# Fused RWKV attention, Mish MLP and greedy MoE on one core: the attention bonus of units 6 to 23 moved from TensorE to VectorE, with a new order of steps

## The chip, the cores and the metric

One core of one Trainium2 chip runs the whole program as a single launch. The metric is device time in microseconds (us), the median of several runs. Engines are named as the profile names them: PE is TensorE (PEld its weight loads), DVE is VectorE, ACT is ScalarE, POOL is GpSimd, SP is the engine that issues most DMAs.

## The reference, cut to what matters

```python
# attention: r, k, v, w are (4 batches, 8 heads, 768 steps, 48), u is (8, 48)
for t in range(S):
    cur = einsum('bhd,bhe->bhde', u[None] * kt, vt)
    y[:, :, t] = einsum('bhd,bhde->bhe', rt, state + cur)
    state = wt[..., None] * state + einsum('bhd,bhe->bhde', kt, vt)
# MLP on x = y as 3072 tokens of 384 features
h = x @ w_in                        # 384 -> 2048
g = h * tanh(softplus(h))
x = g @ w_out                       # 2048 -> 384
# MoE: greedy assignment of tokens to 8 experts, 384 tokens each,
# by falling logit of x @ w_gate, then per expert relu(x @ w1) @ w2
```

The part of y that `cur` gives is the bonus: for one token and one head it is the scalar sum over d of r·u·k, times v of the same token. The change is about how that scalar is computed.

## The kernel before, in words

**Attention.** The 768 steps of a pair of batches are cut into 12 chunks of 64 steps, and a unit is one chunk of one pair: 24 units (`n` from 0 to 23) of 128 tokens and 8 heads. r, k and w arrive with the head dimension on the partitions (`rkw`, 48 of each 64 partitions used), v with the tokens on the partitions (`v`). Steps of a unit: `att0` (a scan of the decay on VectorE, and the product rk = r·k), `att1` (key "r1": a second scan, and r scaled), `att1b` ("k1": k scaled), `bon1` and `bon2` (the bonus), `att_A` ("A1": the 64x64 scores into PSUM, and the masked copy of them over the bonus matrix `Dt`), `att_K` ("K": transposes of k), `att_S` ("S": the state), `att4` ("y": scores times v, then x0 and its remainder written as two f16 halves into `xg`, and the loads of later units).

**The bonus before.** `bon1` multiplies rk by u on TensorE (8 products of 64 columns, which the trace counts as 16 matmuls), one row of PSUM per head, and copies the 128x128 block to `bT`. `bon2` transposes that block on TensorE, copies the 8 useful columns to `bt` (tokens on the partitions), and spreads bt over a diagonal into `Dt`.

**MLP.** Two units make a group of 256 tokens (12 groups). `mm1(g, j)` is slot t = 8g + j: 18 matmuls of 256 columns into a PSUM tile `Hp` (two buffers). ACT reads each tile twice (tanh into `es`, a copy into `hs`; a few copies go to DVE). A half group (4 slots) of `es` then goes through arctan ("at") and sine ("sin") on ACT, `act_he` on DVE multiplies h by the result, and `act_g` writes the high f16 half (on ACT or DVE, by list) and the low half (DVE). `es` has two buffers: the tanh of a half waits until `act_he` of the half before the last has read them. `mm2` is a stream of 384 parts, each 3 matmuls of 384 or 392 columns, handed out between the slots.

**Weights at the start.** w_in and w_out arrive as 64-bit floats in 16 blocks; `conv` (three integer operations on DVE) makes f32 of a block, `split` (one ACT, one DVE) two f16 halves. `og_T` and `og_M` multiply w_out by the gate weights, so that mm2 gives the gate logits as well. `warm(n)` issues n matmuls whose result nobody reads.

**The order.** Every step is an event with a number as its key: the list `CFG` gives the number for each kind of step, the events are sorted by it, and every engine works through its own instructions in that program order. Slot t of mm1 has the key t + 0.689. For units from 6 on, the keys of units n and n+1 repeat every 8 slots. From slot 16 to 81 `beat` says how many mm2 parts follow slot t (by t mod 8). The sets in `CFG['dve']` say which copies run on DVE; the others run on ACT. SP issues nearly all DMAs, in program order, and holds each until its buffer is free.

**After the MLP.** The greedy gate (a chain of short DVE and PE steps, with the last mm2 parts between them), then the eight experts.

```python
t0 = 8 * (n // 2) - 8 if n >= 6 else 4 * n - 13
for nm, o in {**(CFG["u"][n % 2] if n >= 6 else {}), **CFG["un"].get(n, {})}.items():
    at(t0 + o, steps[nm], n)
...
for key, _, f, args in sorted(events, key=lambda x: x[:2]):
    f(*args)
```

Of the kernel before, what the change touches and what calls it, by code (L numbers as in the profile page):

```python
# [23 lines left out]
CFG = {'conv': [-28.468, -27.682, -10.675, -9.847, -2.299, 2.231, 3.277, 4.9, 3.919, 5.933, 7.595, 7.755, 8.526, 9.471,  # L24
          10.454, 11.547],
 'split': [-25.675, -27.076, -3.646, 1.639, 1.676, 2.567, 3.66, 7.281, 4.908, 7.502, 8.011, 9.047, 9.415, 10.573,
           10.811, 12.671],
 'ogT': [5.845, 8.719, 9.555, 9.756, 11.048, 11.752, 12.058, 13.442],
 'ogM': [7.704, 9.381, 9.717, 10.657, 11.711, 12.133, 12.863, 15.308],
 'u': ({'att0': -6.475,  # L30
        'bon1': -2.417,
        'bon2': -1.013,
        'r1': 0.465,
        'k1': -1.596,
        'K': 1.584,
        'A1': 2.502,
        'S': 3.903,
        'y': 3.747},
       {'att0': -2.581,
        'bon1': -0.459,  # L40
        'bon2': 0.009,
        'r1': -0.43,
        'k1': 0.751,
        'K': 5.062,
        'A1': 5.181,
        'S': 5.915,
        'y': 5.938}),
 'un': {0: {'att0': -24.666,
            'r1': -16.321,
            'bon1': -15.996,  # L50
            'k1': -21.723,
            'K': -15.816,
            'A1': -14.582,
            'bon2': -15.13,
            'S': -15.595,
            'y': -13.813},
        1: {'att0': -20.054,
            'r1': -19.91,
            'bon1': -18.88,
            'k1': -18.572,  # L60
# [3 lines left out]
            'S': -16.313,  # L64
            'y': -15.386},
        2: {'att0': -21.397,
            'r1': -20.207,
            'bon1': -20.059,
            'k1': -19.864,
            'bon2': -3.587,  # L70
            'K': 4.356,
            'A1': 3.2,
            'S': 6.8,
            'y': 7.301},
        3: {'att0': -21.601,
            'r1': -18.499,
            'bon1': -0.615,
            'k1': -16.885,
            'bon2': 2.966,
            'K': 3.773,  # L80
            'A1': 6.657,
            'S': 6.652,
            'y': 7.118},
        4: {'K': 5.178,
            'A1': 4.914,
            'S': 5.604,
            'y': 8.165,
            'att0': 0.318,
            'bon1': 1.82,
            'bon2': 4.604,  # L90
            'r1': 3.684,
            'k1': 4.536},
        5: {'y': 7.557,
            'att0': -2.858,
            'bon1': 3.509,
            'bon2': 3.642,
            'r1': 3.498,
            'k1': 1.649,
            'K': 6.184,
            'A1': 5.986,  # L100
            'S': 6.749},
        6: {'att0': -3.536, 'bon1': -2.54, 'bon2': 0.136},
        7: {'att0': -2.822, 'bon1': -0.422, 'bon2': 1.839}},
 'rate': [(17, 1), (16, 18), (77, 192), (80, 194), (96, 224), (99, 245)],
 'beat': (16, 82, (8, 3, 1, 1, 1, 0, 3, 5)),
 'close_cv': 15.533,
 'close_att': 86.65,
# [11 lines left out]
           ('ld', 5): -25.319,  # L119
           ('ld', 6): -18.857,  # L120
           ('ld', 7): -23.785,
           ('ld', 8): -21.26,
# [1 line left out]
           ('warm', 1): -24.585,
           ('warm', 2): -22.903,
           ('warm', 3): -6.441,
           ('warm', 4): 9.117,
           ('warm', 5): 2.921,
# [26 lines left out]
def tile_rwkv_mish_greedy_moe(  # L155
# [185 lines left out]
    def att0(n):  # L341
        if n > 2 and UN[n - 3][1] + 1 < NCH:
            need(("S", n - 3))
        if n > 1:
# [907 lines left out]
def lay_out(x):  # L1252
# [67 lines left out]
```

## Time and profile before

| What | Value |
|---|---|
| median of 3 runs | 784.49 us (783.0 to 786.48) |
| the profiled execution's own time | 783.24 us |
| its span, first to last instruction | 781.5 us |
| PE busy | 733.1 us (94%) |
| DVE busy | 556.6 us (71%) |
| ACT busy | 411.0 us (53%) |
| granted TensorE clock, mean | 0.981 |

The busy shares are averages over stages that have different limits: loading and converting weights while attention starts, a long stretch in which attention and MLP run side by side, the gate, and the experts. What the change is worth is read stage by stage.

### The profile page before, as it was taken

The page shows a single profiled execution, that of the slowest core. Times are in us where ns is not written, and L with a number is a line of the kernel's source. Part 1 is how long each engine was busy: PE and PEld are TensorE (multiplying, and loading weights), DVE is VectorE, ACT ScalarE, POOL GpSimd, SP SyncE. Part 2 cuts the span into 40 slices and gives each one's busy share as a digit, 9 for nine tenths or more (in the row PEclk, how much of TensorE's full clock was granted, in tenths as well). Part 3 has the DMA queues.
Part 4 walks back from the last instruction along what each step waited for, and adds up shares of the span by engine and source line. Part 5 has one row for each costly group of instructions (what it writes and reads, how often), then busy time and mean ns, then how long its engine had stood idle before and what let it go on. Part 6 is the DMA issues. An engine that isn't in the chain of part 4 may idle for free. (4 is left out here: it accounts for less than half of the span.)

```text
span 781.5 us, 20165 instructions
## 1 busy us (share of the span) xinstructions
PE 733.1 (94%) x8807; PEld 517.0 (66%) x8807; DVE 556.6 (71%) x1054; ACT 411.0 (53%) x689; POOL 57.0 (7%) x98
## 2 busy tenths in 40 slices
PE   3977699999999999999999999999979999999996
PEld 2656576878777787777777765555556666666663
DVE  8999996978788887978777446777745664446620
ACT  3365875576774667667576781110024565445621
POOL 0000000000000000000000010000031223312211
PEclk9998899999999999999999999999989999999999
DMA  8852331323133141322210005100525644456100
GB/s 335 247 181 60 125 97 26 68 42 86 45 67 60 40 94 41 70 57 47 53 27 13 5 14 180 22 21 12 183 74 182 213 150 162 167 200 212 52 31 30
DMA packets 22220, 74.12 MB, mean 95 GB/s; under 512 B 4496, under 2 KB 13072, under 8 KB 20080
## 3 DMA queue, kind: packets, MB, share of 16 engines
q1 hardware_dynamic: 19056, 63.35, 27.7%
q0 software_dynamic: 3072, 9.44, 3.8%
q8 instruction: 71, 1.16, 0.6%
q14 instruction: 21, 0.17, 0.1%
HBM read 62.15 MB, written 9.44 MB: 92 GB/s over the span
## 5 line engine op out<-in xcount | busy, mean ns | idle before, releaser
L561 PE MATMUL Hp<-xg,wi 128*128 128x256 f16 x1728 | 210.4, 277 | 3.9 <-ACT wi L504 1.9
L616 PE MATMUL X<-wo,g 128*128 128x392 f16 (+1 forms) x1152 | 211.0, 328 | 0.0
L561 PEld LDWEIGHTS <-wi 128*128 128x128 f16 x1728 | 167.8, 99 | 33.3 <-ACT wi L504 2.1
L616 PEld LDWEIGHTS <-g 128*128 128x128 f16 x1152 | 107.2, 98 | 63.5 <-issue 0.9
L565 ACT ACTIVATE es<-Hp 128x512 f32<-128x512 f32 x96 | 57.4, 597 | 112.8 <-PE Hp L561 80.0
L1167 PE MATMUL X<-a,hT 128*128 128x384 f16 x576 | 97.2, 326 | 0.0
L1150 PEld LDWEIGHTS <-a 128*128 128x128 f16 x612 | 57.8, 98 | 37.2 <-issue 1.2
L1167 PEld LDWEIGHTS <-hT 128*128 128x128 f16 x576 | 56.4, 98 | 34.8
L1150 PE MATMUL Hp<-xe,a 128*128 128x384 f16 (+1 forms) x468 | 74.7, 314 | 0.7 <-DVE xe L1131 0.4
L588 DVE TENSOR_TENSOR hs<-hs,es 128x1024 f32<-128x1024 f32 x48 | 57.6, 1218 | 17.8 <-ACT es L580 17.6
L601 DVE TENSOR_TENSOR g<-hs,g 128x1024 f16<-128x1024 f32 x48 | 58.7, 1224 | 13.1 <-ACT g L329 12.1
L1095 DVE SCALAR_TENSOR_TENSOR a<-stg,a 128x384 f16<-128x384 f32 (+1 forms) x112 | 63.9, 607 | 0.0
L1092 ACT ACTIVATE a<-stg 128x384 f16<-128x384 f32 (+1 forms) x112 | 56.9, 561 | 0.8 <-DMA stg<-in_w_dram 0.8
L1170 ACT ACTIVATE or<-X 128x384 f32<-128x384 f32 x24 | 11.8, 491 | 81.0 <-issue 60.7
L1155 DVE SCALAR_TENSOR_TENSOR hT<-Hp,hT 128x384 f16<-128x384 f32 x48 | 26.4, 551 | 38.7 <-ACT hT L1154 38.7
L1131 DVE SCALAR_TENSOR_TENSOR xe<-cn,xe 128x384 f16<-128x384 f32 x24 | 13.2, 553 | 56.4 <-ACT xe L1130 56.4
L580 ACT ACTIVATE es<-es,right 128x1024 f32<-128x1024 f32 x48 | 53.3, 1153 | 0.2
L329 ACT ACTIVATE x1o<-X 128x384 f32<-128x384 f32 x19 | 9.4, 493 | 81.2 <-PE X L616 41.6
L329 ACT ACTIVATE hs<-Hp 128x512 f32<-128x512 f32 x77 | 46.0, 598 | 9.0 <-DVE g L601 9.0
L573 ACT ACTIVATE es<-es,mid__124 128x2048 f32<-128x2048 f32 x24 | 48.1, 2003 | 0.4
L1116 POOL DMA_INDIRECT xr<-x_dram,idx x24 | 27.5, 1146 | 119.6 <-DVE idx L1067 111.4
L273 ACT ACT_TABLE_LOAD x26 | 33.4, 1283 | 1.2 <-PEq L1304 0.8
(190 smaller groups left out, 881.1 us busy)
## 6 DMA issues: line engine op xcount, KB each, us to landing
stg<-in_w_dram SPq DMA_DIRECT2D x16, 1536.0 KB, 6.8
T<-in_rkw_dram SPq DMA_DIRECT2D x42, 289.5 KB, 4.9
g<-in_w_out_dram SPq DMA_DIRECT2D x8, 768.0 KB, 5.8
v<-in_v_dram SPq DMA_DIRECT2D x24, 192.0 KB, 3.1
x_dram<-x1o SPq DMA_DIRECT2D x48, 96.0 KB, 2.2
g<-in_w_in_dram SPq DMA_DIRECT2D x4, 768.0 KB, 7.9
wo<-in_w_in_dram SPq DMA_DIRECT2D x4, 768.0 KB, 11.6
xg<-xg SPq DMA_DIRECT2D x72, 16.0 KB, 1.9
```

The lines of the kernel that those rows point to most:

```text
L329: nc.scalar.activation(dst, src, AF.Copy, scale=scale)
L561: nc.tensor.matmul(h[:, fi, :], wi[:, a, kk, f * P:(f + 1) * P], xg[g][:, b, kk, :], start=(n == 0), stop=(n == 3 * KD - 1))
L565: nc.scalar.activation(es[g, hf][:, 2 * q:2 * q + 2, :], h, AF.Tanh, scale=0.5 / (SX * SWI))
L573: nc.scalar.activation(e, e, AF.Arctan, scale=-0.5, bias=mid_)
L580: nc.scalar.activation(e, e, AF.Sin, scale=-2.0, bias=right)
L588: nc.vector.tensor_tensor(h, h, e, op=ALU.mult)
L601: (nc.vector if on_v("glo", 2 * H_ + q) else nc.gpsimd).tensor_tensor(gt[:, 1, sl], h, gt[:, 0, sl], op=ALU.subtract)
L616: nc.tensor.matmul(x, gt[:, a, ff, m * P:(m + 1) * P], wo[:, b, f, 0:n], start=(f == 0 and i == 0), stop=(f == NF - 1 and i == 2))
L1092: nc.scalar.activation(dst[:, 0], src, AF.Copy, scale=sc_)
L1095: nc.vector.scalar_tensor_tensor(dst[:, 1], src, sc_, dst[:, 0], op0=ALU.mult, op1=ALU.subtract)
L1150: nc.tensor.matmul(ps[:, cs], a1[:, a, kk, f * P:(f + 1) * P], x[:, b, kk, cs], start=(n == 0), stop=(n == 3 * KD - 1))
L1167: nc.tensor.matmul(ps, h[:, a, f, ms], a2[:, b, f, :], start=(n == 0), stop=(n == 3 * NF2 - 1))
```

## The change

Units 0 to 5 keep the bonus as it was. For units 6 to 23 r and k are fetched a second time, now with the tokens on the partitions, u comes spread over all 128 partitions (`ur`), and DVE forms r·k, times u, and sums each head's 48 numbers. `bon1` does nothing for these units, and `att0` makes no rk. The buffer of the fetched pair is single (`bufs=1`): unit n+1 is fetched once unit n has been summed. v comes out of the same array as r and k. Nearly every key of the order is new; the sets of copies on DVE change as shown. The keys of single steps are left out below but for the bonus of the later units.

```diff
- 'u': ({'att0': -6.475,
-        'bon1': -2.417,
-        'bon2': -1.013,
...
-       {'att0': -2.581,
-        'bon1': -0.459,
-        'bon2': 0.009,
...
+ 'u': ({'att0': -5.987,
+        'bon1': -2.919,
+        'bon2': -1.132,
...
+       {'att0': -3.2,
+        'bon1': -0.255,
+        'bon2': 0.362,
...
- 'beat': (16, 82, (8, 3, 1, 1, 1, 0, 3, 5)),
+ 'beat': (16, 82, (8, 2, 1, 1, 0, 0, 3, 7)),
...
- 'warm': [3, 0, 3, 21, 0, 2, 8],
- 'amount': {'I0': 3, 'I1': 0, 'c': 3, 'g': 1, 'o': 20, 't': 5},
+ 'warm': [10, 0, 3, 17, 4, 2, 16],
+ 'amount': {'I0': 3, 'I1': 0, 'c': 3, 'g': 1, 'o': 26, 't': 5},
...
-         'Dt': {4, 5, 6, 7, 8, 9, 10, 12, 13, 14, 15, 16, 17, 18, 19, 20, 21, 22, 23},
-         'kn': {10, 14},
+         'Dt': {4, 5, 6, 7, 8, 9, 10, 12, 13, 14, 15, 16, 17, 18, 19, 20, 22, 23},
+         'kn': set(),
...
-         'x0': {0, 4, 5, 6, 7, 8, 9, 10, 11, 12, 13, 14, 15, 16, 17, 18, 19, 21, 22, 23},
-         'bT': {9, 6, 14},
-         'wT': {13, 17, 19, 21, 23}},
+         'x0': {0, 5, 7, 9, 11, 13, 15, 17, 19, 21, 23},
+         'bT': {17, 21, 7},
+         'wT': {13, 14, 16, 17, 19, 21, 22}},
...
+ 'nb': 6}
...
-        nc.sync.dma_start(vt[n], v[n])
+        nc.sync.dma_start(vt[n], rkv[n, :, 2])
...
-    u_T = pa.tile([P, NP, 2, 32], F32, name="u_T", bufs=1)
-    nc.sync.dma_start(u_T.rearrange("p a h b -> p (a h b)"), u)
+    uw = pa.tile([P, H * D], F32, name="uw", bufs=1)
+    u_T = uw[:, 0:NP * 64].rearrange("p (a h b) -> p a h b", a=NP, h=2)
+    nc.sync.dma_start(uw[:, 0:NP * 64], u)
+    rkn = {}
+
+    def load_rk(n):
+        if NB <= n < NU:
+            if n == NB:
+                nc.sync.dma_start(uw, ur)
+            rkn[n] = pa.tile([P, 2, H * D], F32, name="rk", bufs=1)
+            nc.sync.dma_start(rkn[n].rearrange("p a (h d) -> p a h d", h=H), rkv[n, :, 0:2])
...
-        rk = pa.tile([P, NP, C], F32, name="rk", bufs=1)
-        nc.vector.tensor_tensor(rk, Tps["r", n], Tps["k", n], op=ALU.mult)
-        rks[n] = rk
+        if n < NB:
+            rk = pa.tile([P, 2, H * D], F32, name="rk", bufs=1).rearrange("p a c -> p (a c)")[:, 0:NP * C]
+            rk = rk.rearrange("p (a c) -> p a c", a=NP)
+            nc.vector.tensor_tensor(rk, Tps["r", n], Tps["k", n], op=ALU.mult)
+            rks[n] = rk
...
     def bon1(n):
+        if n >= NB:
+            return
...
     def bon2(n):
+        if n >= NB:
+            x = rkn[n]
+            nc.vector.tensor_tensor(x[:, 0], x[:, 0], x[:, 1], op=ALU.mult)
+            nc.vector.tensor_tensor(x[:, 0], x[:, 0], uw, op=ALU.mult)
+            bt = pa.tile([P, 2, NP], F32, name="bt")
+            for j in range(2):
+                nc.vector.tensor_reduce(bt[:, j], x[:, 0].rearrange("t (p j d) -> t j p d", p=NP, j=2)[:, j], op=ALU.add,
+                                        axis=AX.X)
+            rkn.pop(n)
+            load_rk(n + 1)
+            bonus_diag(n, bt)
+            return
         pb = pq.tile([P, C], F32, name="Y", bufs=2)
         made.add("whole")
         nc.tensor.transpose(pb, bTs.pop(n), ident)
         bt = pa.tile([P, 2, NP], F32, name="bt")
         move("bT", n, bt, pb.rearrange("t (p j) -> t j p", j=32)[:, 0:2, :])
+        if n == NB - 1:
+            load_rk(NB)
+        bonus_diag(n, bt)
+
+    def bonus_diag(n, bt):
         bt = bt.rearrange("t j p -> t (j p)")
```

In the new order the events of one pair of units (here 12 and 13, slots 38 to 41; `he 8 1` is half 8, second quarter) read: y 11 (37.918), k1 12 (38.448), bon2 12 (38.868), g 7 1 (39.512), r1 13 (39.874), r1 12 (40.131), k1 13 (40.314), bon2 13 (40.362), he 8 0 (40.527), he 8 1 (40.643), mm1 40 (40.689). Before they read: y 11 (37.938), k1 12, bon2 12 (38.987), g 7 1, r1 13, bon2 13 (40.009), he 8 0, r1 12, he 8 1 (40.525), mm1 40 (40.689), k1 13 (40.751).

## Rows read from the trace of the kernel before

**Rows 1.** Windows by stage: length, then busy time of PE, PEld, DVE, ACT, POOL, clock, DMA.

```profile
0.00:107.00 107.00, 75.51 (x1188) 56.81 (x1189) 101.35 (x166) 58.64 (x117) 1.73 (x10) 0.90 0.58 185
107.00:121.65 14.65, 14.15 (x308) 12.42 (x306) 14.18 (x23) 14.05 (x18) 0.00 (x0) 1.00 0.26 58
121.65:412.44 290.79, 289.82 (x4266) 221.63 (x4263) 236.41 (x368) 189.12 (x272) 0.00 (x0) 1.00 0.25 55
```

**Rows 2.** Timeline of PE, one pair of units: start, length, what.

```profile
252.18 0.43 PE L374 MATMUL Y<-rk,u_T 128*32 128x64 f32 x16
252.54 2.14 PE L561 MATMUL Hp<-xg,wi 128*128 128x256 f16 x18
...
256.35 2.14 PE L561 MATMUL Hp<-xg,wi 128*128 128x256 f16 x18
258.32 0.27 PE L381 MATMUL Y<-ident,bT 128*128 128x128 f32 x1
258.43 1.66 PE L616 MATMUL X<-wo,g 128*128 128x392 f16 x9
...
266.92 4.14 PE L616 MATMUL X<-wo,g 128*128 128x392 f16 x24
...
275.98 0.28 PE L561 MATMUL Hp<-xg,wi 128*128 128x256 f16 x1
```

**Rows 3.** Groups by line, whole run: count, busy us, mean ns, idle before.

```profile
L353 DVE TENSOR_TENSOR rk<-T 128x512 f32<-128x512 f32 x24 | 16.0, 667 | 0.5 <-DMA T<-in_rkw_dram 0.5
...
L460 DVE TENSOR_TENSOR S<-S,F 128x384 f32<-128x384 f32 x20 | 11.2, 558 | 0.7
...
L885 DVE TENSOR_REDUCE best<-Vs 128x24 f32<-128x192 f32 x1 | 0.4, 354 | 0.0
...
L1050 DVE TENSOR_REDUCE sl<-scn 128x24 int32<-128x192 f32 x1 | 0.6, 615 | 0.0
...
L327 DVE TENSOR_SCALAR xg<-A 128x512 f16<-128x512 f32 x20 | 13.7, 686 | 1.9 <-PE A L473 1.8
```

**Rows 4.** Window of one pair, 240.91 to 274.88 us: columns as in rows 1.

```profile
240.91:274.88 33.97, 33.77 (x509) 26.14 (x508) 29.07 (x48) 21.10 (x29) 0.00 (x0) 1.00 0.31 60
```

**Rows 5.** Timeline of DVE in that pair.

```profile
258.60 0.76 DVE L480 SCALAR_TENSOR_TENSOR xg<-A,xg 128x256 f16<-128x256 f32 x2
259.27 0.68 DVE L397 TENSOR_TENSOR T<-T,F 128x512 f32<-128x512 f32 x1
...
262.54 0.20 DVE L358 RECIPROCAL first<-F 128x8 f32<-128x8 f32 x1
...
264.66 0.68 DVE L327 TENSOR_SCALAR hs<-Hp 128x512 f32<-128x512 f32 x1
...
271.01 1.22 DVE L588 TENSOR_TENSOR hs<-hs,es 128x1024 f32<-128x1024 f32 x1
```

**Rows 6.** Timeline of ACT in that pair.

```profile
272.32 0.60 ACT L565 ACTIVATE es<-Hp 128x512 f32<-128x512 f32 x1 [3.57 <-DVE hs L588]
```

**Rows 7.** Timeline of SP in that pair.

```profile
259.38 4.71 SPq L486 DMA_DIRECT2D xg<-xg  x6
```

**Rows 8.** The page's DMA issues: count, KB each, us to landing.

```profile
g<-in_w_out_dram SPq DMA_DIRECT2D x8, 768.0 KB, 5.8
v<-in_v_dram SPq DMA_DIRECT2D x24, 192.0 KB, 3.1
```

**Rows 9.** Timeline of PE, start of the run and the last mm2 parts of the gate.

```profile
2.01 1.46 PE L339 MATMUL Y<-id 128*128 128x512 f16 x3 [2.01 <-DVE id L281]
6.85 0.66 PE L374 MATMUL Y<-rk,u_T 128*32 128x64 f32 x16 [3.38 <-DVE rk L353]
...
562.14 5.04 PE L616 MATMUL X<-wo,g 128*128 128x384 f16 x30
```

**Rows 10.** Timeline of DVE at the end of the weight conversion.

```profile
108.55 1.23 DVE L350 TENSOR_TENSOR_SCAN F<-T,first 128x520 f32<-128x520 f32 x1
...
111.41 0.95 DVE L505 SCALAR_TENSOR_TENSOR wo<-cv,wo 128x768 f16<-128x768 f32 x1
```

More of the change, by code (lines that the diff above doesn't have):

```diff
@@ L21 @@
 SEQ = 768
-CFG = {'conv': [-28.468, -27.682, -10.675, -9.847, -2.299, 2.231, 3.277, 4.9, 3.919, 5.933, 7.595, 7.755, 8.526, 9.471,
+CFG = {'conv': [-28.468, -28.233, -10.675, -9.847, -3.389, 2.249, 3.447, 4.661, 4.089, 5.933, 7.237, 7.743, 8.526, 9.495,
           10.454, 11.547],
[L26 to L29, printed above, removed]
- 'u': ({'att0': -6.475,
-        'bon1': -2.417,
-        'bon2': -1.013,
[L33 to L38, printed above, removed]
-       {'att0': -2.581,
-        'bon1': -0.459,
-        'bon2': 0.009,
[L42 to L57, printed above, removed]
@@ new lines @@
+ 'split': [-26.085, -27.173, -3.643, 0.741, 1.676, 2.651, 3.66, 6.008, 4.915, 7.723, 8.006, 9.047, 9.486, 10.78,
+           10.805, 12.671],
+ 'ogT': [5.759, 8.781, 9.555, 10.425, 11.079, 11.844, 11.926, 13.193],
+ 'ogM': [7.758, 9.334, 9.771, 10.781, 11.786, 12.209, 12.731, 15.188],
+ 'u': ({'att0': -5.987,
+        'bon1': -2.919,
+        'bon2': -1.132,
+        'r1': 0.131,
+        'k1': -1.552,
+        'K': 2.028,
+        'A1': 2.608,
+        'S': 3.787,
+        'y': 3.844},
+       {'att0': -3.2,
+        'bon1': -0.255,
+        'bon2': 0.362,
+        'r1': -0.126,
+        'k1': 0.314,
+        'K': 4.482,
+        'A1': 5.149,
+        'S': 5.569,
+        'y': 5.918}),
@@ L58 @@
+ 'un': {0: {'att0': -24.617,
+            'r1': -16.818,
+            'bon1': -16.145,
+            'k1': -21.676,
+            'K': -15.719,
+            'A1': -14.474,
+            'bon2': -15.081,
+            'S': -15.546,
+            'y': -13.72},
+        1: {'att0': -20.203,
             'r1': -19.91,
-            'bon1': -18.88,
-            'k1': -18.572,
+            'bon1': -18.764,
+            'k1': -18.426,
             'K': -16.839,
@@ L63 @@
             'bon2': -18.264,
[L64 to L83, printed above, removed]
@@ L84 @@
-        4: {'K': 5.178,
-            'A1': 4.914,
-            'S': 5.604,
[L87 to L102, printed above, removed]
@@ L103 @@
-        7: {'att0': -2.822, 'bon1': -0.422, 'bon2': 1.839}},
- 'rate': [(17, 1), (16, 18), (77, 192), (80, 194), (96, 224), (99, 245)],
- 'beat': (16, 82, (8, 3, 1, 1, 1, 0, 3, 5)),
- 'close_cv': 15.533,
+            'S': -16.335,
+            'y': -15.249},
+        2: {'att0': -21.418,
+            'r1': -19.974,
+            'bon1': -19.617,
+            'k1': -19.64,
+            'bon2': -3.61,
+            'K': 4.997,
+            'A1': 3.276,
+            'S': 6.922,
+            'y': 7.451},
@@ new lines @@
+        3: {'att0': -21.269,
+            'r1': -17.288,
+            'bon1': -0.568,
+            'k1': -15.337,
+            'bon2': 3.561,
+            'K': 3.783,
+            'A1': 6.667,
+            'S': 6.009,
+            'y': 7.234},
+        4: {'K': 5.214,
+            'A1': 4.95,
+            'S': 5.604,
+            'y': 7.836,
+            'att0': 0.608,
+            'bon1': 1.856,
+            'bon2': 4.294,
+            'r1': 3.706,
+            'k1': 4.57},
+        5: {'y': 7.485,
+            'att0': -2.727,
+            'bon1': 3.512,
+            'bon2': 3.756,
+            'r1': 3.755,
+            'k1': 1.907,
+            'K': 6.014,
+            'A1': 5.811,
+            'S': 6.972},
@@ L107 @@
+        6: {'att0': -2.91, 'bon1': -1.909, 'bon2': -0.152},
+        7: {'att0': -1.529, 'bon1': -0.364, 'bon2': 0.748}},
+ 'rate': [(17, 1), (16, 18), (79, 187), (80, 182), (96, 211), (98, 233)],
+ 'beat': (16, 82, (8, 2, 1, 1, 0, 0, 3, 7)),
+ 'close_cv': 15.882,
  'close_att': 86.65,
  'mm1': 0.689,
[7 rows of a table removed]
[7 rows of a table added]
  'begin': {('warm', 0): -39.92,
@@ L118 @@
            ('ld', 4): -26.686,
[L119 to L122, printed above, removed]
+           ('ld', 5): -25.313,
+           ('ld', 6): -16.304,
+           ('ld', 7): -23.746,
+           ('ld', 8): -20.836,
            ('ld', 9): -20.908,
[L124 to L128, printed above, removed]
+           ('warm', 1): -24.627,
+           ('warm', 2): -20.713,
+           ('warm', 3): -7.535,
+           ('warm', 4): 6.922,
+           ('warm', 5): 0.758,
            ('warm', 6): 3.3},
- 'warm': [3, 0, 3, 21, 0, 2, 8],
- 'amount': {'I0': 3, 'I1': 0, 'c': 3, 'g': 1, 'o': 20, 't': 5},
+ 'warm': [10, 0, 3, 17, 4, 2, 16],
+ 'amount': {'I0': 3, 'I1': 0, 'c': 3, 'g': 1, 'o': 26, 't': 5},
  'dve': {'lg': set(),
@@ L158, in tile_rwkv_mish_greedy_moe @@
     rkw: bass.AP,
-    v: bass.AP,
+    rkv: bass.AP,
     u: bass.AP,
+    ur: bass.AP,
     w_in: bass.AP,
@@ L168, in tile_rwkv_mish_greedy_moe @@
     nc = tc.nc
-    NU, C, H, D = v.shape
+    NU, C, _, H, D = rkv.shape
     L = C // 2
@@ L214, in tile_rwkv_mish_greedy_moe @@
     UN = [divmod(n, NCH) for n in range(NU)]
+    NB = CFG["nb"]
     vt = {}
@@ L1286, in lay_out @@
         "rkw": np.concatenate([units(x["w"], 1.0, 1), units(x["r"], 0.0, 0), units(x["k"], 0.0, 0)], axis=2),
-        "v": x["v"].reshape(B // 2, 2, H, NCH, L, D).transpose(0, 3, 1, 4, 2, 5).reshape(NU, C, H, D),
+        "rkv": np.stack([x[a].reshape(B // 2, 2, H, NCH, L, D).transpose(0, 3, 1, 4, 2, 5).reshape(NU, C, H, D)
+                         for a in "rkv"], axis=2),
         "u": u.reshape(P, NP * 64),
+        "ur": np.broadcast_to(x["u"].reshape(1, H * D), (P, H * D)),
         "w_in": w_in,
```

6 lines of the change are left out of this document (3 added, 3 removed), and 18 rows, old and new, of the table CFG.

## The prediction

> **What bounds the kernel now.** I read the windows by stage first, because the shares of the page mix stages with different limits. Up to 107 us DVE works 101.35 of 107 us while PE works 75.51: the start hangs on VectorE, which converts the weights. From 107 to 121.65 us all three engines are nearly full. From 121.65 to 412.44 us, where attention and MLP run side by side, PE is busy 289.82 of 290.79 us at the 2.4 GHz level (granted clock 1.00), DVE 236.41 (81%), ACT 189.12 (65%) [rows 1]. Behind that stand the end of the MLP, the gate and the experts, in which no unit's bonus runs.
>
> A modelled end can make PE look full, so the second view is the timeline of PE, by its starts. A slot of mm1 goes from 256.35 to 258.32 us: 18 matmuls of 256 columns in 1.97 us, 109 ns each, where 256 columns at 2.4 GHz are 107 ns. There is no gap to hide in: what is taken out of PE's queue between 121.65 and 412.44 us moves everything behind it forward, as long as PE is not made to wait for something else. The Trainium skill, page "Trainium Kernel Development and Optimization", section "Performance Expectations", says the opposite of trusting that row: matmul busy time is a bad measure, the busy share of weight loads a good one. That share is 221.63 of 290.79 us, 76%, here; by it a quarter of the stretch would be slack and the removal could be hidden, which is the third rival below. The starts, 109 ns apart, speak against it.
>
> **What is removed from PE.** The 16 matmuls of `bon1` start at 252.18 and the next work at 252.54 us: 0.36 us. The transpose of `bon2` starts at 258.32 and the next work at 258.43: 0.11 us [rows 2]. Together 0.47 us for a unit, and 18 units lose both: 18 x 0.47 = 8.5 us. Sixteen of these lie in the full stretch; units 6 and 7, by their old keys (13.46 and 15.58), lie just ahead of it, between 107 and 121.65 us, where PE is busy 14.15 of 14.65 us [rows 1], so I count them too. Bounds: 16 units, 7.5 us; 18 units, 8.5 us.
>
> The copies bT and bt leave ACT, which is no limit at 65%, and leave the PSUM tiles Y to K and S. I count nothing for it.
>
> **What is added to DVE.** For each unit two products of 384 elements and two sums of 192. The product is priced by the 384-element product of `att_S`, 558 ns; the sum by the reduction of 192 elements to 24, 354 ns; one other reduction of 192, with strides and an integer result, took 615 ns and is the upper bound. Added: 2 x 0.558 + 2 x 0.354 = 1.82 us (2.35 at the upper bound). Removed: rk, 0.67 us [rows 3]. Net 1.16 us a unit, 2.3 us a pair. For 7 of the even units behind unit 6 the x0 copy (0.69 us, rows 3) goes to ACT, so a pair gains 1.6 us of DVE work: 29.07 us of 33.97 before [rows 4] becomes about 30.7 of 33.0, 93%. So VectorE still fits, but its waits must shrink from 4.9 to 2.3 us a pair. The skill's "VectorE: DVE Perf Modes", section "Rules for kernel authors", speaks against the change: it calls `tensor_reduce` the slowest DVE operation and advises to keep operations few. The row of 354 ns, against 558 ns for twice the elements in a product, does not show a reduction slower than a product of its size; the rule's side of it is the upper bound above.
>
> **Where DVE can hold PE.** The tight place of a pair is ahead of mm1 of slot 42. There ACT waited 3.57 us, until 272.32 us, for `act_he` (the `es` buffer), then read the Hp tile in 0.60 us [rows 6], and a second time, which I take as long; `act_he` itself ended at 272.23 [rows 5]. PE wanted that tile at 275.98 us [rows 2]. Some 2.5 us were spare.
> In the new order, counted from the end of unit 11's x0 remainder (258.60 + 0.76 = 259.36 us, rows 5), DVE does k1 (0.68), the sums of bon2 12 (1.82), its Dt (0.69), a low half (1.22), a copy of hs (0.68), two r1 (2 x 2.12, from 262.54 to 264.66), k1 (0.68): 10.0 us to the first product of bon2 13. Then 1.82 + 0.69, and two `act_he` of 1.22: 15.0 us, so 274.3 instead of 272.23 us, and the Hp tile is free at 275.5. (All durations are those of rows 3 and 5; the low half and Dt are taken as long as the `act_he` and the copy of their size. Rows 5 start up to 0.1 us before the one ahead has ended, so this is the slow reading.)
> PE's way from 256.35 to 275.98 us gets one mm2 part more (20 instead of 19 by the two `beat` lists; 4.14 / 8 = 0.52 us, 24 matmuls are 8 parts) and loses a `bon1` and two transposes (0.36 + 0.22) [rows 2]: it is there at 275.9 us. So 0.4 us remain spare, about 1.1 with the overlap. At the upper price of the sums two units add 1.05 us, and PE would stand up to 0.6 us a pair.
>
> **The fetch.** Unit 13's r and k can be fetched only when unit 12's sums are read, at 259.36 + 0.68 + 1.82 = 261.9 us. On SP the fetch stands behind six copies of xg, issued until 259.38 + 4.71 = 264.1 us [rows 7], and takes 0.35 us to issue (estimate, as one v load). 384 KB lie between the v load (192 KB, 3.1 us) and a w_out block (768 KB, 5.8 us) [rows 8]; between them, 4.0 us (estimate). It lands at 268.4 us; DVE asks for it at 269.4. So it is hidden by 1 us; at 5.8 us it is 0.8 us late and may cost 0.4. Queued behind it on SP are stores of x1 and loads two units ahead, with slack; the xg copies, which mm1 needs, wait for a later DVE step anyway. The other fetch of a pair has six slots.
> I take 0.1 us a pair for late arrivals of either kind, 1 us for 9 pairs; bounds 0 and 5.4 (0.6 a pair).
>
> **The start.** Up to the last split DVE has two pieces less: the decay scan and rk of unit 6 (1.23 us in rows 10, and 0.67), which now stand behind it, and x0 of unit 4 (0.69): 2.6 us. That split ended at 112.36 us [rows 10], when PE was already full, so most of it is not on the path; and the other steps are reordered in ways that I can't price. I take 0, bounds -2.6 and +3. Fifteen more warm matmuls: seven of them join the first three, which took 1.46 us at 2.01 us; ten end at about 6.9, where the next PE work begins at 6.85 [rows 9]. The others fall where DVE holds PE. Nothing.
>
> **The rest.** Counted through `rate` and `beat`, 250 parts of mm2 come ahead of the gate instead of 251; the first "o" step of the gate gives out what is left, 10 parts before (30 matmuls at 562.14 us, rows 9) and 11 after. The larger limit of 26 has nothing to give. One part moved, same sum. The 7 MB of second fetches meet DMA engines busy 25% of the stretch [rows 1].
>
> **Sum.** -8.5 + 1.0 + 0 = -7.5 us. From the profiled execution's own 783.24 us this is 775.7; the median of the runs shown lies 1.25 us above it, so 777.0 on the median of 784.49. No change that can be told is within 0.5%, 780.6 to 788.4 us.
>
> **Rivals.**
> *VectorE takes the gain back.* If the lateness at `act_he` exceeds the spare 0.4 to 1.1 us by 0.94 us a pair, PE stands as long as it saved: 9 x 0.94 = 8.5, result 784.5. For it: the spare time, which shrinks from 2.5 us, and both upper bounds (sums of 615 ns, a fetch of 5.8 us). Against it: they must come together. Chance 0.13.
> *VectorE becomes the bound (slower).* One mechanism: the single buffer of r and k. From the point where the fetch takes more than about 6.5 us to land, DVE stands at bon2 of the odd unit longer than all spare time; at 8 us it is 3 us late, PE loses 1.9 to 2.6 us a pair against 0.94 saved: +9 to +15 us, about 796. Against it: the medians of rows 8, and DMA engines at 25%. Chance 0.08.
> *The removal is hidden.* By the weight-load share PE would have slack and nothing is won: 784.5. Against it the starts of rows 2. Chance 0.05.
> *The start gains as well.* DVE's 2.6 us ahead of the last split come through, no stall in the pairs: -8.5 - 2.6, 773.4. Chance 0.15.
> The forecast itself has 0.59.
>
> **Numbers.** Faster by over 0.5%: the forecast with 0.59 less 0.04 for its edge near 780.6, and the start's 0.15: 0.70. Within 0.5%: 0.13 + 0.05 + 0.04: 0.22. Slower: 0.08. The range goes from 772 (the last rival and a run's spread) to 784.5, which takes in the bound of 5.4 us of stalls with 3 us lost at the start (784.4).
>
> **What would show it.** In the profile after: PE still over 99% busy from slot 16 to the end of attention, that stretch shorter by about 7 us, and no L374 or L381 after unit 5; the sums near 0.35 us and the products near 0.56; DVE near 90% there; no wait of the product of bon2 for the fetch over 1 us; ACT's wait for `act_he` ending later within a pair but PE not idle ahead of mm1. The forecast is wrong if PE shows idle time in every pair, named after ACT's tanh or the fetch, or if the start ends later than 121.65 us by some us.

## The result, and the profile after

| | before | after |
|---|---|---|
| median of four runs each | 785.19 us | 771.97 us |
| lowest to highest | 783.0 to 786.48 | 771.6 to 773.33 |
| the profiled execution's own time | 783.24 | 771.61 |
| its span | 781.5 | 769.8 |

The ratio is 0.9838, 95% interval 0.9811 to 0.9865: 13.2 us less between the medians, 11.6 us between the two profiled executions. The forecast was 7.5 us less, 777.0; 771.97 lies on the lower edge of the range, 0.03 us below the 772 that it names.

The marks at which the spans part: the first output matmul (mm2) starts at 118.06 us instead of 121.65 (3.59 less); the stretch from there to the scores of unit 22 takes 282.36 us instead of 290.79 (8.43 less); from there to the gate 66.38 instead of 66.49, gate 96.20 instead of 96.16, experts 206.80 instead of 206.41. So the time came out of the two stages in which units 6 to 23 have their bonus. The other 1.6 us of the 13.2 lie between executions: the profiled one is 1.95 us under its median before, 0.36 after.

Windows by stage of the kernel after, as in [rows 1], and as the last line a window as long as one pair takes, to be read beside [rows 4] (length, busy time of PE, PEld, DVE, ACT, POOL, clock, DMA share, GB/s):

```profile
0.00:104.00 104.00, 78.17 (x1222) 56.92 (x1223) 99.75 (x164) 59.35 (x118) 1.72 (x10) 0.83 0.63 196
104.00:118.06 14.06, 13.65 (x259) 11.70 (x256) 11.33 (x19) 11.71 (x15) 0.00 (x0) 0.91 0.25 60
118.06:400.42 282.36, 280.61 (x3989) 215.46 (x3986) 252.18 (x415) 191.99 (x258) 0.00 (x0) 1.00 0.34 80
235.67:267.92 32.25, 32.25 (x477) 25.13 (x475) 29.52 (x50) 22.72 (x31) 0.00 (x0) 1.00 0.36 83
```

PE works 280.61 of 282.36 us: 1.75 us idle, 0.97 before [rows 1], although DVE went from 81% to 89%. In the pair shown PE has no idle time at all, with DVE at 92%.

What PE waited for in that stretch, us in total, times, longest (with "issue" and PEld left out this list is complete):

```profile
PE Hp L677 <- DVE g L634: 0.7, 1, 0.7
PE Hp L594 <- ACT hs L341: 0.5, 1, 0.5
PE A L506 <- DVE Dt L455: 0.3, 1, 0.3
```

Timeline of PE in the pair of units 12 and 13, as in [rows 2]; between `mm1` (L594) and mm2 (L649) no bonus and no transpose of one stands any more:

```profile
247.34 2.14 PE L594 MATMUL Hp<-xg,wi 128*128 128x256 f16 x18
249.32 1.66 PE L649 MATMUL X<-wo,g 128*128 128x392 f16 x9
250.81 2.13 PE L594 MATMUL Hp<-xg,wi 128*128 128x256 f16 x18
252.78 3.65 PE L649 MATMUL X<-wo,g 128*128 128x392 f16 x21
...
266.79 1.48 PE L594 MATMUL Hp<-xg,wi 128*128 128x256 f16 x12
```

Groups by line of the added work, as in [rows 3]; the last row is the old bonus's transpose, now 6 times instead of 24:

```profile
L401 DVE TENSOR_REDUCE bt<-rk 128x4 f32<-128x192 f32 x36 | 11.0, 348 | 0.6
...
L398 DVE TENSOR_TENSOR rk<-rk,uw 128x384 f32<-128x384 f32 x18 | 10.0, 558 | 0.6
L397 DVE TENSOR_TENSOR rk<-rk 128x384 f32<-128x384 f32 x18 | 9.9, 552 | 0.0
...
L409 PE MATMUL Y<-ident,bT 128*128 128x128 f32 x6 | 2.3, 384 | 3.9 <-DVE S L489 3.6 <-DVE S L491 0.3
```

Timeline of DVE in the same pair, as in [rows 5]: the first unit's sums, the second unit's from 260.05 us, then `act_he`, two instructions:

```profile
249.77 0.76 DVE L513 SCALAR_TENSOR_TENSOR xg<-A,xg 128x256 f16<-128x256 f32 x2
250.44 0.68 DVE L430 TENSOR_TENSOR T<-T,F 128x512 f32<-128x512 f32 x1
251.04 0.55 DVE L397 TENSOR_TENSOR rk<-rk 128x384 f32<-128x384 f32 x1
251.62 0.56 DVE L398 TENSOR_TENSOR rk<-rk,uw 128x384 f32<-128x384 f32 x1
252.22 0.61 DVE L401 TENSOR_REDUCE bt<-rk 128x4 f32<-128x192 f32 x2
...
260.05 0.55 DVE L397 TENSOR_TENSOR rk<-rk 128x384 f32<-128x384 f32 x1
...
262.48 2.35 DVE L621 TENSOR_TENSOR hs<-hs,es 128x1024 f32<-128x1024 f32 x2
```

ACT behind it, as in [rows 6], with its wait in brackets:

```profile
264.93 0.60 ACT L598 ACTIVATE es<-Hp 128x512 f32<-128x512 f32 x1 [5.75 <-DVE hs L621]
265.42 0.59 ACT L341 ACTIVATE hs<-Hp 128x512 f32<-128x512 f32 x1
```

ACT now waits 5.75 us for `act_he` instead of 3.57, and PE still has its tile: the second read ends at 266.0, PE asks at 266.79. SP's queue in the pair, as in [rows 7]; its second line joins two fetches of r and k, the first issued at 254.55 us:

```profile
250.59 3.87 SPq L519 DMA_DIRECT2D xg<-xg  x6
254.55 7.65 SPq L270 DMA_DIRECT2D rk<-in_rkv_dram  x2
```

The page's DMA issues, as in [rows 8] (count, KB each, median us to landing):

```profile
rk<-in_rkv_dram SPq DMA_DIRECT2D x18, 384.0 KB, 3.1
v<-in_rkv_dram SPq DMA_DIRECT2D x24, 192.0 KB, 3.0
```

PE at the start and its last mm2 parts in the gate, as in [rows 9]: ten warm matmuls, and 33 matmuls where 30 stood.

```profile
2.01 4.45 PE L351 MATMUL Y<-id 128*128 128x512 f16 x10 [2.01 <-DVE id L293]
...
550.00 5.52 PE L649 MATMUL X<-wo,g 128*128 128x384 f16 x33
```

DVE at the last weight split, as in [rows 10]: it ends at 107.97 us, 4.39 us earlier than before.

```profile
107.02 0.95 DVE L538 SCALAR_TENSOR_TENSOR wo<-cv,wo 128x768 f16<-128x768 f32 x1
```

### The profile page after: what moved, and what is told of

Read it like the earlier page. It is cut to its first block, busy times and chain, and to the rows that moved or that the text cites. A ratio compares the mean times of both kernels' runs of the same rounds, so it can differ in the third digit from the quotient of the medians.

```text
span 769.8 us, 19665 instructions
## 1 busy us (share of the span) xinstructions
PE 726.8 (94%) x8516; PEld 511.0 (66%) x8516; DVE 566.8 (74%) x1091; ACT 414.0 (54%) x677; POOL 57.3 (7%) x98
## 5 line engine op out<-in xcount | busy, mean ns | idle before, releaser
L594 PE MATMUL Hp<-xg,wi 128*128 128x256 f16 x1728 | 209.3, 277 | 2.2 <-DMA xg<-xg 1.6
L649 PE MATMUL X<-wo,g 128*128 128x392 f16 (+1 forms) x1152 | 209.7, 329 | 0.0
L594 PEld LDWEIGHTS <-wi 128*128 128x128 f16 x1728 | 168.7, 99 | 31.4 <-DMA xg<-xg 2.0
L649 PEld LDWEIGHTS <-g 128*128 128x128 f16 x1152 | 107.2, 98 | 64.4
## 6 DMA issues: line engine op xcount, KB each, us to landing
wo<-in_w_in_dram SPq DMA_DIRECT2D x4, 768.0 KB, 12.3
```

Source lines behind the costliest of these rows:

```text
L594: nc.tensor.matmul(h[:, fi, :], wi[:, a, kk, f * P:(f + 1) * P], xg[g][:, b, kk, :], start=(n == 0), stop=(n == 3 * KD - 1))
L649: nc.tensor.matmul(x, gt[:, a, ff, m * P:(m + 1) * P], wo[:, b, f, 0:n], start=(f == 0 and i == 0), stop=(f == NF - 1 and i == 2))
```

## The experiments

Two measures return below. A *period* is the time from the scores of one even unit to those of the next, taken from PE's timeline; the eight periods from unit 6 to 22 are 33.31 33.30 33.55 33.97 33.36 33.41 35.40 35.39 before and 32.26 32.39 32.34 32.25 32.26 32.57 35.35 34.55 after, 7.72 us less, 0.97 a pair on average (from 0.05 to 1.72). The *start* is the time of the first mm2 part. Three pairs of kernels that are the same up to that point differ by 0.9, 1.1 and 2.8 us in it (118.06 and 117.15; 122.04 and 120.92; 122.09 and 124.86), so no difference of some 2 us is read from two starts alone. The granted clock has a part in that. One and the same slot, in the kernel after (0.91 from 104 us to the start) and in the last kernel below (1.00):

```profile
104.02 3.35 PE L594 MATMUL Hp<-xg,wi 128*128 128x256 f16 x18
...
104.33 2.13 PE L594 MATMUL Hp<-xg,wi 128*128 128x256 f16 x18
```

Ratios are to the kernel before on the same chip.

### The new bonus in the old order

The changed program with the whole `CFG` of before, `nb` added.

```diff
-CFG = {...}                       # the changed kernel's
+CFG = {..., 'cvn': 2, 'nb': 6}    # that of before, with nb
```

> The new bonus (units 6 to 23 on VectorE) in the old order with the old lists. Theory 1 (the gain of the long stretch is the PE work taken out, 0.47 us a unit, whatever the order): 785.2 - 8.5 = 776.7 us, or up to 779 if the odd unit's fetch is late, since in the old order VectorE asks for it about 2 us earlier. Theory 2 (the gain of the long stretch is the new order's, the bonus alone only trades PE time for VectorE stalls): 784 to 790. The start, up to the first mm2 parts, should stay near 121 us under both (units 6 and 7 leave PE 0.7 us there).

Measured: 783.99 us, ratio 0.9995 (0.9981 to 1.0008). The bonus alone wins nothing. Periods 32.26 34.10 35.61 32.67 33.23 33.55 36.10 35.05: some pairs are as short as in the new order, two near unit 11 are far longer. ACT there:

```profile
199.38 2.02 ACT L424 ACTIVATE Dt<-diag,bt 128x64 f32<-128x64 f32 x8 [3.53 <-DVE bt L401]
```

And PE:

```profile
207.28 0.70 PE L447 MATMUL A<-T 48*64 48x64 f32 x32 [1.77 <-DVE T L378]
...
209.59 4.00 PE L594 MATMUL Hp<-xg,wi 128*128 128x256 f16 x18 [1.15 <-ACT hs L341]
```

The reader is to see a chain: unit 11's `Dt` is one of the few left to ACT (11 is not in that set). Its input now comes late, from DVE; ACT stands 3.53 us with its sines queued behind, DVE's `act_he` then waits 4.28 us for the sines, and PE waits 1.77 and 1.15 us. And the 18 matmuls of the slot behind take 4.00 us instead of 2.14. The windows of 4 us each, the first from 0.7 us ahead of it, go with that: the granted clock is 0.50, the 1.2 GHz level, and then 0.68.

```profile
208.92:212.92 4.00, 3.33 (x16) 2.31 (x16) 2.23 (x4) 4.00 (x8) 0.00 (x0) 0.50 0.37 83
212.92:216.92 4.00, 4.00 (x25) 2.68 (x22) 3.81 (x5) 1.96 (x3) 0.00 (x0) 0.68 0.57 118
```

### The same with `Dt` of unit 11 on DVE

```diff
-  'Dt': {4, 5, 6, 7, 8, 9, 10, 12, ...
+  'Dt': {4, 5, 6, 7, 8, 9, 10, 11, 12, ...
```

> The new bonus in the old order, as the first run of it, with one copy more on VectorE: the diagonal of unit 11 (Dt), which in that run stood on ScalarE behind the late sums and held PE for 1.8 + 1.2 us, with the granted clock at 0.50 to 0.68 in the 8 us behind it. Theory 1, mended (what is taken from PE is gained where PE is kept fed, and a wait of PE of some 2 us costs about twice its length, since the clock falls behind it): that pair's two periods, 34.1 and 35.6 us, go to about 33, and the time from 784 to about 779. Theory 2 (the order as a whole decides, this copy doesn't): 783 to 785.

Measured: 778.37 us, ratio 0.9906 (0.9876 to 0.9935), periods 32.25 32.26 32.76 33.14 33.24 33.29 36.01 35.05. One number in one set brought 5.6 us between the medians, 7.0 by the ratios (the two runs were on different chips), of the 13: the chain above was the cause of that part. Left over are 4.12 us of idle PE in the stretch (282.77 busy of 286.89) and a start of 120.92 us.

### The new order with the old bonus

```diff
- 'nb': 6}
+ 'nb': 24}
```

> The new order and lists with the old bonus for all units. Theory 1: 772.0 + 8.5 = 780.5 us, a period of a pair of 33.3 us as before, and a start about 3 us shorter than before. Theory 2: 772 to 775, with the period of a pair near 32.3 us.

Measured: 808.96 us, ratio 1.0317 (1.0295 to 1.034). Neither theory holds: with the old bonus the order costs 25 us. In the profiled execution (801.5 us, the shortest of six) PE waits 13.8 us in six pieces for the copy `bT`, 2.30 each: `att_S` needs the PSUM tile Y that `bon1` has filled, and ACT comes to empty it late, because ahead of `bT` a copy of hs waits for DVE (2.38 us in the pair below). The timeline of ACT:

```profile
186.78 0.60 ACT L341 ACTIVATE hs<-Hp 128x512 f32<-128x512 f32 x1 [2.38 <-DVE g L634]
187.27 0.27 ACT L341 ACTIVATE bT<-Y 128x128 f32<-128x128 f32 x1
```

The timeline of PE there, and three pairs later:

```profile
187.59 0.68 PE L484 MATMUL Y<-v,kn 64*64 64x48 f32 x30 [2.30 <-ACT bT L341]
188.20 2.14 PE L594 MATMUL Hp<-xg,wi 128*128 128x256 f16 x18
...
292.04 0.90 PE L484 MATMUL Y<-v,kn 64*64 64x48 f32 x30 [2.30 <-ACT bT L341]
292.87 3.52 PE L594 MATMUL Hp<-xg,wi 128*128 128x256 f16 x18
```

The 4 us behind each of these two waits, by window:

```profile
187.59:191.59 4.00, 4.00 (x87) 3.40 (x88) 2.90 (x5) 2.09 (x4) 0.00 (x0) 1.00 0.30 71
...
292.04:296.04 4.00, 4.00 (x47) 3.07 (x48) 2.31 (x4) 0.89 (x1) 0.00 (x0) 0.57 0.34 60
```

The wait is the same to 0.01 us, but behind the second the clock is granted at 0.57: those 4 us do 2.3 us of work at full clock, so that the wait cost 2.3 + 1.7 us (estimate). It adds up: the stretch to the scores of unit 22 takes 308.86 us, 18.1 more than before, with 13.0 us more idle time of PE, and 5.1 us more in which it is busy, which is three times 1.7.

### The same with the old bonus's own keys

Here `bon1` and `bon2` stand where they stood before, but for `bon1` of even units, which goes to -3.25, and the set `bT` is that of before.

```diff
- 'nb': 6}
+ 'nb': 24}
-        'bon1': -2.919,
+        'bon1': -3.25,
-  'bT': {17, 21, 7},
+  'bT': {9, 6, 14},
...
```

> The new order with the old bonus, now with the old keys and the old copies of the bonus steps (bon1 of even units moved just ahead of the odd unit's decay scan, since it shares the rk buffer). Theory 1, mended: periods of 33.3 us again and no large waits, a start that is shorter by 2 to 3 us: 781 to 783 us. Theory 2 (the new order carries the gain): below 777. If a wait of PE for the copy bT stays in each pair, as in the run with untouched keys: above 795.

Measured: 809.11 us, ratio 1.0312 (1.028 to 1.0344). The waits for `bT` stay (11.5 us, five of 2.30). So the old keys of the bonus steps don't bring the old bonus back to its time in the new order; its tile still has to be emptied by ACT, which is late there. Whether keys exist that would, wasn't tried.

### Half of the units

Units 6 to 13 with the old bonus, 14 to 23 with the new, in the new order.

```diff
- 'nb': 6}
+ 'nb': 14}
```

> The new order, with the old bonus for units 0 to 13 and the new one for 14 to 23. Theory 1: 8 units give back 0.47 us each, 772.0 + 3.8 = 775.8 us; periods of 33.3 us up to unit 13 and 32.3 us behind it. Theory 2: 772 to 773, all periods alike.

Measured: 784.12 us, ratio 0.999 (0.9974 to 1.0007), outside both theories. Periods 33.42 37.49 32.64 32.26 32.25 32.79 35.18 34.54, start 124.86: pairs with the new bonus (from the fourth period on) are those of the kernel after, and the loss is in the start (6.8 us) and in the three periods of units 8 to 13, which keep the old one (103.55 us against 96.99, 6.6).

### One more product on DVE in every unit

A useless product of 384 elements into the unused half of the fetched tile, 0.55 us a unit, 1.1 a pair.

```diff
+            nc.vector.tensor_tensor(x[:, 1], x[:, 1], uw, op=ALU.mult)
             bt = pa.tile([P, 2, NP], F32, name="bt")
```

> The changed kernel with one useless product of 384 elements (0.55 us) more in each later unit, 1.1 us a pair on VectorE. By the trace of the changed kernel PE reaches mm1 of slot 42 about 0.8 us after its Hp tile is free. Theory S (that spare time is all there is): PE stands about 0.3 us a pair, 772 + 2.7 = 775 us, more if the clock falls behind the waits. Rival (VectorE's idle 30 us in the stretch absorb it): within 1 us of 772.

Measured: 775.52 us, ratio 0.9882 (0.9853 to 0.9911), 3.5 us above the kernel after. That is the time of Theory S, but not its picture of 0.3 us in every pair. In the pair shown the spare time of 0.8 us shrinks to 0.1 and PE doesn't stand; in three other pairs it does (0.43, 0.76 and 1.08 us), at the place that the prediction named, the tile of `mm1` (L595; lines stand one further here). By the periods (32.26 32.74 32.55 32.34 32.26 34.10 36.19 34.65) two pairs pay nothing and one pays 1.5 us. PE's waits in the stretch:

```profile
PE Hp L595 <- ACT hs L341: 1.2, 2, 0.8
PE Hp L595 <- DVE hs L339: 1.1, 1, 1.1
PE Hp L678 <- DVE g L635: 1.0, 1, 1.0
```

PE's idle time there is 4.48 us (280.94 busy of 285.42) against 1.75, 2.7 of the 3.5 us.

### x0 of the even units back on DVE

```diff
-         'x0': {0, 5, 7, 9, 11, 13, 15, 17, 19, 21, 23},
+         'x0': {0, 4, 5, 6, ..., 18, 19, 21, 22, 23},
```

> The changed kernel with the products x0 of nine even units (4, 6, 8, 10, 12, 14, 16, 18, 22) back on VectorE, as the kernel before has them: the 0.69 us a pair that the change had taken off VectorE are put on again, nothing is left out. Theory A (what counts is the spare time at the end of the pair's VectorE work, 0.8 us by the changed kernel's trace): 0.69 lies within the spare, so at most a wait of a few tenths in some pairs, 772 to 773.5 us. Rival B (every tenth of a microsecond on VectorE costs, in the proportion in which the useless product of 1.1 us a pair cost 3.5 us): 774.2 us. Rival C (the product is asked for early in the unit and delays the first half's work rather than the last): the periods of the pairs grow by 0.3 us and more, above 775 us.

Measured: 773.26 us, ratio 0.9861 (0.9839 to 0.9883; the kernel after 0.9811 to 0.9865). The intervals overlap, and the time is the one that Theory A gave. The pairs are not: by the periods (32.26 32.38 33.05 32.26 32.25 33.19 36.09 34.54) five pairs pay nothing and three 0.6 to 0.7 us, 2.05 us in all. The spare time covers the product in most pairs, and where it doesn't, nearly all of it is paid. PE's longest new wait, 0.64 us ahead of the scores of unit 11, is for `xg` from DVE: there it isn't the spare time at the tile of `mm1` that counts.

### The fetch cut in sixteen

The fetch of r and k as 16 transfers of 24 KB, which makes it later, and with it what SP issues behind it.

```diff
-  nc.sync.dma_start(rkn[n]..., rkv[n, :, 0:2])
+  for c in range(0, P, 8):
+      nc.sync.dma_start(rkn[n][c:c + 8]..., rkv[n, c:c + 8, 0:2])
```

> The changed kernel with each fetch of r and k cut into 16 transfers of 8 partitions, so that SP needs about 16 x 0.37 = 6 us instead of 0.4 to issue it. In the trace of the changed kernel the odd unit's fetch is issued at 254.55 us, lands about 3.1 us later and is asked for at 260.05: 2.4 us early. Cut up it lands near 263, some 3 us late. The prediction's slower rival (a late fetch stalls VectorE, and PE behind it, in every pair): 9 x 2.2 = 20 us longer, 790 to 800 us, more with the clock. If VectorE's wait is absorbed: 772 to 776.

Measured: 784.26 us, ratio 0.9994 (0.9975 to 1.0013), 12.3 us above the kernel after. Waits in the stretch (lines stand one further here too):

```profile
DVE rk L398 <- DMA rk<-in_rkv_dram: 12.4, 7, 2.8
...
PE Hp L595 <- ACT hs L342: 4.9, 3, 2.9
...
PE Hp L595 <- DVE hs L340: 3.6, 2, 1.9
```

The slower rival's chain exists as it was told (late fetch, DVE, tanh's tile, PE), with PE idle 11.9 us (283.41 of 295.32). DVE waited for seven of the 18 fetches, not for one in every pair, so it cost less than the 790 to 800 us of that rival, and more than the 776 of the other. DVE also waits 7.4 us for the loads `T`, 1.6 in the kernel after, so part of the 12 us may be theirs.

### Two more DVE pieces at the start

x0 of unit 4 back on DVE, and the scan of unit 6 ahead of the last split again: 1.9 us of the 2.6 that the prediction counted.

```diff
-         'x0': {0, 5, ...
+         'x0': {0, 4, 5, ...
-        6: {'att0': -2.91, ...
+        6: {'att0': -3.536, ...
```

> The changed kernel with two VectorE pieces put back ahead of the last weight split: the decay scan of unit 6 (1.2 us) and the x0 copy of unit 4 (0.7 us); rk of unit 6 stays out. Theory A (VectorE's work ahead of the last split sets the end of the start): first mm2 parts about 1.8 us later, 773.8 us. Theory B (PE is full by then, the pieces are covered; the start's gain has another cause): within 0.5 us of 772.0.

Measured: 773.12 us, ratio 0.9866 (0.9849 to 0.9883), between the two theories; the ratios can't tell it from the kernel after. The last split ends at 110.28 us, 2.3 later, and the start is at 118.37, only 0.3 later. PE does wait for the split here, 0.41 us, which it doesn't in the kernel after:

```profile
110.34 0.68 PE L557 MATMUL X<-id,wo 128*128 128x128 f16 x9 [0.41 <-DVE wo L538]
```

But a wait of the same length behind it, 0.41 us for `S` at 115.65 us, is gone. So of the 2.3 us of the split little reaches the start.

### The start's four lists exchanged, in both directions

The positions of `conv`, `split`, `og_T` and `og_M`, lists of before in the changed kernel, and lists of after in the old order with the new bonus and `Dt` of unit 11 on DVE.

```diff
- 'split': [-26.085, -27.173, -3.643, 0.741, 1.676, 2.651, 3.66, 6.008, ...
+ 'split': [-25.675, -27.076, -3.646, 1.639, 1.676, 2.567, 3.66, 7.281, ...
...
```

> The changed kernel with the four lists of the start (the positions of the convolution, of the weight splits and of the output gate's steps) from the kernel before; the positions of the first eight units and all the rest stay as changed, nothing is left out. Theory A (the start's gain beyond the bonus of units 6 and 7, some 2.9 us, is these lists' doing, the last weight split standing 4 us earlier): first output matmul at 120.9 us as in the old order with the new bonus, 774.5 to 775 us. Rival B (it is the first units' positions and the number of warm-up matmuls): first output matmul stays at 118 to 118.5 us, 772 to 772.5 us.

> The old order with the new bonus and Dt of unit 11 on VectorE (778.4 us before, first output matmul at 120.9 us) with the four lists of the start from the changed kernel; nothing is left out. Theory A (these lists carry the start's gain): first output matmul at 118 to 118.5 us, 775.5 to 776.5 us. Rival B (they do not): it stays at 120.5 to 121.5 us, 778 to 779 us; the lists' keys fit the other units' keys of the new order, so a loss is possible as well: above 779.5 us.

Measured: starts of 119.69 and 119.26 us; 771.91 us (ratio 0.9838, 0.9814 to 0.9863) and 776.99 (0.9905, 0.988 to 0.993). In both directions the lists move the start by some 2 us: up from 118.06 and 117.15, down from 122.04 and 120.92. Like kernels differ by as much, so the starts alone don't show it, and the total times don't either. PE's waits do. From 66 us to the start they sum to 11.5 to 12.9 us in the four kernels with the old lists, and to 8.9 to 10.9 in the seven with the new bonus and the new lists. With the old lists the waits for `kn` (4.29 us), for a weight split (1.71) and for `bT` (2.12), named below for the kernel before, are back in the new order; with the new lists in the old order only that for `bT` (2.28) stays. Neither theory holds alone. With `Dt` of unit 11 and these lists the old order is still 5 us above the kernel after; which of the other keys and sets bring these, wasn't taken apart.

### `Dt` of units 11 and 21 on DVE in the new order

```diff
-  'Dt': {4, 5, 6, 7, 8, 9, 10, 12, ..., 20, 22, 23},
+  'Dt': {4, 5, 6, 7, 8, 9, 10, 11, 12, ..., 20, 21, 22, 23},
```

> The changed kernel with the step Dt of units 11 and 21 on VectorE as well, where it takes about 1.1 us, instead of on ScalarE, where it takes about 2 and stood 6.2 us (two times) behind the late sums; nothing is left out. Theory A (the two ScalarE steps still hold back the middle tiles of their pairs): the periods of those two pairs fall, 770.5 to 771.5 us. Rival B (in the new order ScalarE has the time, so the wait ends in idle time of ScalarE and costs nothing, and VectorE's 1.1 us in two pairs eat the spare): 771.7 to 773 us.

Measured: 770.76 us (769.43 to 771.52), ratio 0.9832 (0.9811 to 0.9852). It is the fastest kernel of the study, but not to be told from the kernel after by the ratios. The profile speaks for a small gain, as Theory A had it: the period of units 10 and 11 is 31.36 us instead of 32.34 (that of 20 and 21 stays), PE's idle time in the stretch 0.88 us instead of 1.75.

```profile
117.15:398.38 281.23, 280.35 (x3989) 215.39 (x3986) 253.28 (x417) 188.16 (x242) 0.00 (x0) 1.00 0.33 80
```

## Why the prediction came out as it did

**PE is the bound of the stretch: right.** The third rival, that the removal is hidden behind slack that the weight loads' 76% suggests, fell: the periods lost 0.97 us on average where the slots by PE's starts had said 0.94. The Trainium skill's rule on busy time ("Trainium Kernel Development and Optimization", "Performance Expectations"), read as that rival reads it, would have kept the time at 784.5; here the spacing of the starts was the better guide.

**What is removed, -8.5 us: right in size.** 7.72 us in eight periods. The stretch as a whole lost 8.43: in it one mm2 part fewer runs (612 matmuls counted, 615 before), which moved into the gate, where PE has time and the stage kept its 96.2 us. The prediction had "one part moved, same sum"; by the row of 24 matmuls in 4.14 us it is some 0.5 us gained. PE's busy time in the stretch fell by 9.21 us, and the timelines place nearly all of it: 16 `bon1` of 0.36 us, 5.8; 18 transposes of 0.11 us, 2.0, for those of units 6 and 7 lie in the stretch (130.60 and 139.06 us) and not ahead of it as the prediction read; the part, 0.5; and 0.7 which the prediction missed, because nine mm2 matmuls ahead of a `bon1` took 1.59 us to its start and ahead of an `mm1` take 1.49, eight times.

**What DVE pays: right.** Sums of 348 ns where 354 was taken, products of 552 and 558 ns where 558 was; the upper bound of 615 was idle. DVE at 92% of a pair (93% said), though the busy time of that pair rose only from 29.07 to 29.5 us, not to 30.7, since other copies moved as well; over the whole stretch it rose by 15.8 us, 1.75 for each of nine pairs, where 1.6 was said. The Trainium skill ("VectorE: DVE Perf Modes", "Rules for kernel authors") calls the reduction the slowest operation; 348 ns for 192 elements, as long as an addition of 192 (`S`, L491, 348 ns), shows nothing of that here, and it is the spare time that decided.

**The place where DVE can hold PE, and its spare time: right.** 0.8 us in the pair shown (said: 0.4 to 1.1). With 1.1 us more a pair PE stands at that very place, though in three pairs only and not in the one shown; with 0.69 more, three pairs of eight pay, and mostly at other places. So the spare time differs from pair to pair, and that the sum for 1.1 us came out at 3.5 is in part luck. Rival one would have needed some 1.7 us more a pair (0.8 and the 0.94 saved); the upper price of the sums was 1.05.

**The fetch: right, with more room.** It was issued at 254.55 us and, at the median of 3.1 us, there at 257.7; DVE asked at 260.05. Hidden by 2.4 us instead of 1, because 384 KB landed in 3.1 us, not 4.0, as fast as v's 192 KB. Rival two's chain was made by hand and costs 12 us, but a transfer in one piece is far from it.

**Give-back of 1.0 us: too large.** PE's idle time in the stretch grew by 0.8 us, at places of which one only, of 0.5 us, is the one meant; five of the first six periods are within 0.15 us of the shortest, 32.25.

**The start, 0 us: the term that was wrong.** It gained 3.6 us in the profiled execution. The step that failed is "That split ended at 112.36 us [rows 10], when PE was already full, so most of it is not on the path; and the other steps are reordered in ways that I can't price. I take 0". Its first half is right in the main: PE waited 0.49 us for that split before, and with the two DVE pieces put back the start was 0.3 us later. So the rival "the start gains as well", near to the result in its number (773.4), had the wrong mechanism. The second half was where the gain lay. Two of PE's waits before, the largest and the one for the last split:

```profile
81.24 1.10 PE L451 MATMUL Y<-v,kn 64*64 64x48 f32 x32 [3.75 <-ACT kn L329]
...
112.42 0.68 PE L524 MATMUL X<-id,wo 128*128 128x128 f16 x9 [0.49 <-DVE wo L505]
```

PE's waits in its timeline between 66 us and the start sum to 12.9 us before and 10.6 after, 2.3 us less; the largest before were 3.75 us for `kn` on ACT at 81.24, 2.13 for `bT` at 96.42 and 1.91 and 1.71 us for a weight split at 69.99 and 72.08, a split that the new order places earlier. Two units' `bon1`, 0.72 us, are the second part. By the exchange of lists the first of these parts, about 2 us, is theirs. The gain needs the bonus off PE as well: with the old bonus in units 6 and 7 the same new order starts at 122.09, 124.13 and 124.86 us. There PE waits for DVE ahead of `bon1`, and the slot behind is slow; in the first of these runs:

```profile
114.24 0.43 PE L390 MATMUL Y<-rk,uw 128*32 128x64 f32 x16 [2.92 <-DVE S L491]
...
115.48 3.47 PE L594 MATMUL Hp<-xg,wi 128*128 128x256 f16 x18
```

So the PSUM tiles Y, for which the prediction counted nothing, had a price in the new order. Which single step carries the rest stays open, and the sum of the waits is no full account of a start: in the run with half of the units it is 10.6 us as in the kernel after, and the start 6.8 us later, with the granted clock at 0.73 from 104 us on.

**What the prediction did not see.** It read the change as a sum of parts: so much PE work less, the order only rearranged. The parts don't add. The bonus alone is worth nothing that can be told (ratio 0.9995), or 7 us with one copy moved (0.9906); the order alone costs 25 us; both together win 13. My own first theory behind the result, that the removed PE work would be won in any order, fell with the first experiment. For the stretch the prediction's working held because it went through DVE's queue in the new order, step by step, and there found it fitting.

## What to carry to other kernels

Work taken off a full engine is won only where the order keeps that engine fed: look in the new order for the next consumer of each result that is now made later, and on which engine it stands; one copy left on the wrong engine ate 7 us of 13 here, by the ratios. Price added work by the spare time at the one place where it can hold the bound engine, not by its engine's share: 89% busy cost nothing, and 1.1 us a pair more cost 3.5 in all; and read that spare time in every pair, not in one. And in a start where PE is not full, list its waits rather than take "not priced" as nothing.

## What the runs showed of the hardware

A wait of PE can cost up to about twice its length (estimate: 2.30 us and the 1.7 us lost in the 4 us at 0.57; 2.9 us in two waits and about as much lost at 0.50 and 0.68). In the new order with the old bonus six waits of 2.30 us (2.31 once) were followed by 4 us at a granted clock of 1.00 (at 187.59, 256.13 and 406.62 us) or at 0.57 (at 292.04, 329.55 and 367.08), and the 18 matmuls of the next slot took 2.14, or 3.52 to 3.57 us. In the old order with the new bonus, waits of 1.77 and 1.15 us were followed by 0.50 and 0.68, and a slot of 4.00 us. What tells the waits that lose the clock from those that don't, these runs don't show.

A fetch of 384 KB landed in 3.1 us (2.9 to 5.4), as 192 KB did in 3.0: between these sizes the median landing time hardly grew here (768 KB took 5.6 and more).
